# Three-part attention, routing and MLP kernel: side work between engines, the first load in three, MLP blocks of three tiles, and shifted ranks

## The chip, the cores and the metric

One core of a Trainium2 chip runs the whole program. The metric is device time in microseconds (us) of one execution, lower is better. The engines are TensorE (PE, matmuls and transposes, with weight loads as PEld), VectorE (DVE), ScalarE (ACT), GpSimd (POOL) and SyncE (SP, which issues most DMAs).

## The reference, cut to what matters

Three stages follow each other, on 4 sequences of 768 rows and 384 columns.

```python
# 1. gated linear attention, 8 heads of 48
state = alpha[:, :, t, :, None] * state + einsum('bhd,bhe->bhde', k[:, :, t], v[:, :, t])
y[:, :, t] = einsum('bhd,bhde->bhe', q[:, :, t], state)
# 2. four attention experts of width 64, the best two of four per row
q, k, v = x @ wq[e], x @ wk[e], x @ wv[e]
a = softmax(causal(scale * (q @ k.T)))
out += (e among the top 2) * w * (a @ v @ wo[e])
# 3. MLP, hidden width 1536
xn = (x - mean) / sqrt(var + 1e-6) * g_ln
return x + max(xn @ w_ch1, 0) @ w_ch2
```

## The kernel before, in words

Rows are worked on in tiles of 128, six to a sequence, 24 in all. Most matmul operands are split into a high and a low part (names ending in H and L or h and l), and a product is three matmuls: high by high, low by high, high by low.

*Front.* For each chunk `c` of 128 rows, `gla_a` makes the running product of alpha on DVE (the scan, L383), its logarithm and inverse on ACT (L386, L387), the product gm (L390, POOL, for the first chunk DVE), two steps on k (L392, L394, DVE) and the product on q (L396, POOL). `gla_b` makes the scores on PE in half-array mode (L415), masks them on DVE (`smk`, L422) and transposes k. `gla_c` updates the state (quarter-array matmuls L454; DVE adds; POOL multiplies by the decay, L471) and makes the output (L482), which DVE and ACT split into `xh`, `xl` (L509). For two chunks at a time, `qkv` projects (L539 with 256 columns, L560 with 260), and a chain of small operations makes the gate weights `W`.

*Attention units.* A unit `u` is one tile of queries and one pair of experts, 48 in all. `scores` makes the scores (L649); with more than four tiles of keys they come in two halves of 320 or 384 columns, and such a unit is called wide here. DVE takes row maxima and masks (L658, L660), ACT the exponentials (L664), and POOL makes `rr`, the gate weight over the sum, spread over 64 columns (L676). `transp` transposes exponentials and `rr` (L703), and either ACT or DVE copies them out (L709, L710). `av` multiplies by v (L732, quarter-array mode), DVE scales (L743), ACT takes the high part `oh` (L747) and POOL the low part `ol` (L748). `wout` projects both units of a tile (L759) and the result goes to DRAM.

*MLP.* Weights are converted on the way (`conv`, DVE, ACT and POOL). Blocks of rows follow: two of 256 rows (`NS = 2`) and five of 512. `mlp_tr` transposes (L893), `mlp_1` is the first layer (L919, with as many columns as the block has rows), `mlp_2` the second (L938, 384 columns, for each tile of the block). Small blocks may run among the units of the last sequence; the big ones need the memory of the attention.

*Order.* Nothing is issued as it is written. Every operation is recorded with a rank, `pos` (the PE time recorded before it), its cost in ns and the tiles that it reads and writes. `Plan.run` then walks through a model of the engines: on each it takes, among the operations that can start first, the one of lowest rank (on PE with a preference for the array mode in use), and issues it. An operation may have an alternative on a second engine, `alt`, and goes to the one where the model ends it first; before, only the copies L709 and L710 have that. While DVE holds an operation marked `lock`, a POOL operation is made to wait for it.

## Time and profile before

| | |
|---|---|
| median of 3 runs | 651.92 us (649.41 to 652.05) |
| profiled execution | 648.84 us, its span 647.1 us |
| TensorE clock granted | 1.000 of full speed |
| PE busy | 626.6 us, 6988 matmuls |
| DVE busy | 423.5 us, 1205 instructions |
| ACT busy | 282.7 us, 771 instructions |
| POOL busy | 160.1 us, 265 instructions |
| DMA | 60.93 MB, 94 GB/s on average |

The span runs from the first to the last instruction of the core. A busy PE is one with a matmul in flight, and ends of matmuls are modelled, so gaps of less than a matmul's own length between two of them do not show as idle. A matmul of 32-bit floats that is not in the split form stands in the trace as two.

### The profile page before, as it was taken

The page shows a single profiled execution, that of the slowest core. Times are in us where ns is not written, and L with a number is a line of the kernel's source. Part 1 is how long each engine was busy: PE and PEld are TensorE (multiplying, and loading weights), DVE is VectorE, ACT ScalarE, POOL GpSimd, SP SyncE. Part 2 cuts the span into 40 slices and gives each one's busy share as a digit, 9 for nine tenths or more (in the row PEclk, how much of TensorE's full clock was granted, in tenths as well). Part 3 has the DMA queues.
Part 4 walks back from the last instruction along what each step waited for, and adds up shares of the span by engine and source line. Part 5 has one row for each costly group of instructions (what it writes and reads, how often), then busy time and mean ns, then how long its engine had stood idle before and what let it go on. Part 6 is the DMA issues. An engine that isn't in the chain of part 4 may idle for free.

```text
span 647.1 us, 16965 instructions
## 1 busy us (share of the span) xinstructions
PE 626.6 (97%) x6988; PEld 574.9 (89%) x6988; DVE 423.5 (65%) x1205; ACT 282.7 (44%) x771; POOL 160.1 (25%) x265
## 2 busy tenths in 40 slices
PE   7899999999999999989899999999999999999997
PEld 6789999999988999878898998898898899899897
DVE  6999999999999988799997544424414324331311
ACT  4448565746766655676664422302402311320200
POOL 4475553546444443422223100000000000000000
PEclk9999999999999999999999999999999999999999
DMA  9445243634554223495231201011011011000001
GB/s 347 160 149 198 94 134 104 226 102 143 187 191 129 84 72 103 114 311 169 62 94 61 69 25 36 2 62 36 1 50 49 1 40 58 1 13 37 2 13 37
DMA packets 30430, 60.93 MB, mean 94 GB/s; under 512 B 2960, under 2 KB 19856, under 8 KB 30352
## 3 DMA queue, kind: packets, MB, share of 16 engines
q1 hardware_dynamic: 18864, 45.68, 21.5%
q10 hardware_dynamic: 8352, 9.44, 4.2%
q0 software_dynamic: 3136, 4.72, 2.7%
q8 instruction: 55, 0.90, 0.6%
q14 instruction: 23, 0.19, 0.1%
HBM read 45.67 MB, written 14.16 MB: 92 GB/s over the span
## 4 chain that ended last, share of the span: by engine, by line
PE 65%; DVE 3%; ACT 1%; issue 1%; POOL 0%; DVEq 0%; POOLq 0%
PE F L919 24%; PE F L938 23%; PE F L732 3%; PE F L703 3%; PE F L539 3%; PE F L759 2%; PE F L649 2%; PE F L560 2%; PE F L893 1%; PE F L482 1%; ACT A L664 1%; DVE mx L658 0%; DVE smk L422 0%; DVE gt L383 0%; PE F L454 0%
## 5 line engine op out<-in xcount | busy, mean ns | idle before, releaser
L919 PE MATMUL F<-Nh,w1hl 128*128 128x512 f32 x360 | 93.7, 395 | 0.0
L923 ACT ACTIVATE Hh<-F 128x512 fp32r<-128x512 f32 x60 | 36.0, 600 | 128.6 <-PE F L919 128.6
L924 DVE SCALAR_TENSOR_TENSOR Hl<-F,Hh 128x512 fp32r<-128x512 f32 x60 | 41.5, 691 | 74.4 <-ACT Hh L923 74.4
L919 PEld LDWEIGHTS F<-Nh,w1hl 128*128 128x128 f32 x360 | 67.6, 188 | 15.8
L938 PE MATMUL F<-w2h,Hh 128*128 128x384 f32 x240 | 81.7, 340 | 0.0
L938 PE MATMUL F<-w2h,Hl 128*128 128x384 f32 x240 | 80.7, 336 | 0.0
L938 PE MATMUL F<-w2l,Hh 128*128 128x384 f32 x240 | 80.6, 336 | 0.0
L664 ACT ACTIVATE A<-F,nm 128x384 f32<-128x384 f32 (+4 forms) x128 | 68.2, 543 | 24.3 <-DVE nm L660 20.5
L946 DVE TENSOR_TENSOR xt<-F,xt 128x384 f32<-128x384 f32 x24 | 13.3, 556 | 87.6 <-PE F L938 87.6
L703 PE MATMUL F<-ident,A 128*128 128x128 f32 x336 | 51.4, 276 | 5.3 <-ACT A L664 2.6
L919 PE MATMUL F<-Nl,w1hl 128*128 128x512 f32 x180 | 51.7, 396 | 0.0
L703 PEld LDWEIGHTS F<-ident,A 128*128 128x128 f32 x336 | 38.8, 140 | 10.2 <-ACT A L664 3.7
L938 PEld LDWEIGHTS F<-w2l,Hh 128*128 128x128 f32 x240 | 45.2, 188 | 0.0
L938 PEld LDWEIGHTS F<-w2h,Hh 128*128 128x128 f32 x240 | 45.1, 188 | 0.0
L938 PEld LDWEIGHTS F<-w2h,Hl 128*128 128x128 f32 x240 | 45.1, 188 | 0.0
L732 PE MATMUL F<-at,V 128*32 128x128 f32 x1344 | 44.1, 274 | 0.5 <-ACT A L664 0.5
L919 PEld LDWEIGHTS F<-Nl,w1hl 128*128 128x128 f32 x180 | 33.8, 188 | 8.2
L709 ACT ACTIVATE at<-F 128x384 f32<-128x384 f32 (+2 forms) x72 | 35.7, 517 | 11.1 <-PE F L703 10.8
L732 PEld LDWEIGHTS F<-at,V 128*32 128x32 f32 x1344 | 35.4, 109 | 4.5 <-issue 1.5
L482 PE MATMUL F<-smk,vb 128*32 128x128 f32 x768 | 33.9, 273 | 2.1 <-DVE smk L422 2.1
L676 POOL TENSOR_TENSOR rr<-den,W 128x128 f32<-128x128 f32 x48 | 19.1, 399 | 66.0 <-DVE den L674 24.0
L396 POOL TENSOR_TENSOR ld<-ld,gt 128x512 f32<-128x512 f32 (+1 forms) x26 | 29.1, 1118 | 20.1 <-DVE gt L383 13.0
(196 smaller groups left out, 1461.0 us busy)
## 6 DMA issues: line engine op xcount, KB each, us to landing
ld<-in_akq_dram SPq DMA_DIRECT2D x24, 770.0 KB, 4.9
vb<-in_vd_dram SPq DMA_DIRECT2D x24, 256.0 KB, 5.0
raw<-in_w_dram SPq DMA_DIRECT2D x18, 256.0 KB, 2.9
wsc<-whl ACTq DMA_DIRECT2D x18, 256.0 KB, 3.6
xs<-xo ACTq DMA_DIRECT2D x24, 192.0 KB, 2.1
raw<-in_w_dram SPq DMA_DIRECT2D x12, 384.0 KB, 3.2
w1hl<-wsc POOLq DMA_DIRECT2D x4, 1152.0 KB, 11.9
xt<-xs SPq DMA_DIRECT2D x24, 192.0 KB, 2.5
```

What stands on the lines that cost most here:

```text
L396: op("POOL", 1150 if m == 512 else 896, lambda js=js, q=q: pool.tensor_tensor(q(), q(), gt()[:, js, 1:], op=OP.mult), r=gts + kq, w=kq, na ...
L482: pe.matmul(o, l[x][0], l[x][1], start=(x == 0), stop=(x == len(l) - 1), skip_group_check=True)
L539: pe.matmul(P2()[:, mt % 2], wt()[:, k, cs], x()[:, k], start=(n == 0 and k == 0), stop=(n == 2 and k == 2))
L664: op("ACT", t_act(pw) + 200, lambda h=h, x=x: act.activation(A[h]()[:, pw * x:pw * x + pw], P[h][x]()[:, :pw], AF.Exp, bias=nm()[:, h:h + ...
L676: op("POOL", 360, lambda: pool.tensor_tensor(rr(), den()[:, :, None].to_broadcast([128, 2, 64]), W()[:, i, 2 * p:2 * p + 2, None].to_broad ...
L703: pe.transpose(P()[:, 128 * n:128 * n + 128], a, ident)
L709: fa = lambda cs=cs, P=P, n=n: act.activation(at()[:, cs], P()[:, :n], AF.Copy)
L732: pe.matmul(O()[64 * h + y:64 * h + y + ws], V()[:, x, HD * e + y:HD * e + y + ws], at()[:, c:c + 128], start=(x == 0), stop=(x == i), ski ...
L919: pe.matmul(P()[:, :n], t()[:, w, k, c], x()[:, k], start=(m == 0), stop=(m == 8))
L923: op("ACT", t_act(n) + 63, lambda P=P, hh=hh: act.activation(hh(), P()[:, :n], AF.Relu), r=[P], w=[hh], name="hh")
L924: op("DVE", t_dve(n), lambda P=P, hh=hh, hl=hl: dve.scalar_tensor_tensor(hl(), P()[:, :n], 0.0, f(hh()), op0=OP.max, op1=OP.subtract), r=[ ...
L938: pe.matmul(P()[:, :DM], x()[:, o], W2[w]()[:, ff], start=(ff == 0 and n == 0), stop=(ff == KF - 1 and n == 2))
```

## The change

The code changes in seven ways.

1. *Side work.* The q and gm products of the first two chunks go to DVE (`GD = 2`). The state's decay, two POOL operations of 48 partitions, becomes four of 112 partitions by 96 columns on ACT, each with POOL as the alternative (`SGA = 2`). `rr` and `ol` stay on POOL with DVE as the alternative (`RRA = 2`, `OLA = 1`). A subtraction on POOL in the gate chain becomes the bias of ACT's exponential, one for each tile instead of one for two. Clearing of `hot` and the states moves from POOL to DVE, and what waited for the whole of POOL's setup now waits for the part it reads.
2. *First load.* Chunk 0 comes in three transfers, the alpha part first, then k, then q.
3. *Finer waits.* Projections and scores wait for tiles of 128 rows instead of pairs.
4. *MLP blocks* of 2, 2, 2 and then six of 3 tiles. Their input loads are recorded earlier, and those of the three-tile blocks wait for the attention's memory.
5. *Six* warm-up groups on PE instead of ten, each with a higher cost.
6. *Cost* of a DMA's completion 2300 ns instead of 1900.
7. *Ranks.* `reorder` adds to `pos` of chosen groups of operations among the first 2600 a random shift, from thirty seeds (`ORDER`); `Plan.run` then picks by that `key`.

```diff
+BLOCKS = (2, 2, 2, 3, 3, 3, 3, 3, 3)
+SGA = 2
+RRA = 2
+GD = 2
+ORDER = (53, 71, 74, 129, 134, 144, 149, 254, 384, 385, 443, 714, 717, 1188, 1460, 2556, 3984, 10423, 11494, 13357, 14198, 14530, 17028, 17166, 17434, 17884, 18058, 20628, 21730, 22753)
+NW = 6
+OLA = 1
...
+    def reorder(self, seeds):
+        ops = self.ops[:2600]
+        for seed in seeds:
+            rnd = random.Random(seed)
+            mid = rnd.uniform(0, len(ops))
+            width = rnd.choice((60, 150, 400))
+            sigma = rnd.choice((400, 1500, 4000))
+            kind = rnd.choice((0, 1, 2))
+            group = {}
+            for o in ops[int(max(0, mid - width)):int(mid + width)]:
+                k = (o.name, o.name + o.plain[0], o.n)[kind]
+                if k not in group:
+                    group[k] = float(round(rnd.gauss(0, sigma))) if rnd.random() < (1, 0.5, 0.25)[kind] else 0.0
+                o.shift += group[k]
...
-                           key=lambda x: (x[1].pos + (STICK if x[1].mode != mode else 0.0), x[1].n))
+                           key=lambda x: (x[1].key + (STICK if x[1].mode != mode else 0.0), x[1].n))
...
-                o.end = chan + 1900.0
+                o.end = chan + 2300.0
...
+        for x, o, n in (("a", 0, AW), ("k", AW + 512, 512), ("q", AW, 512)):
+            op("SP", 400, lambda o=o, n=n: sp.dma_start(L()[:, o:o + n], akq[b, s][:, o:o + n]), w=[(L, (x, j)) for j in range(4)],
+               nbytes=512.0 * n, name=f"ld{c}")
...
-            ge, gn = (dve, "DVE") if c < 1 else (pool, "POOL")
+            ge, gn = (dve, "DVE") if c < max(GD, 1) else (pool, "POOL")
...
+            qe, qn = (dve, "DVE") if c < GD else (pool, "POOL")
...
+            for j in range(4 if SGA and s else 0):
+                gs = lambda j=j: (new_()[:112, j], new_()[:112, j], gt()[:112, j, 128:129])
+                sa = lambda gs=gs: act.activation(*gs()[:2], AF.Copy, scale=gs()[2])
+                sp_ = lambda j=j: pool.tensor_tensor(new_()[:112, j], new_()[:112, j], gt()[:112, j, 128:129, None].to_broadcast([112, 3, 32]), op=OP.mult)
+                op("ACT", 270, sa, r=[(gt, j), (new_, 0), (new_, 1)], w=[(new_, ("g", j))], name=f"stg{c}",
+                   alt=("POOL", 300, sp_, True) if SGA > 1 else None)
...
+            if RRA:
+                op("POOL", 360, lambda: m(pool), r=[den, (W, i)], w=[rr], name="rr", alt=("DVE", t_dve(128), lambda: m(dve), True) if RRA > 1 else None)
...
+        op("POOL", 420, lambda: lo(pool), r=[rb, (oh, p)], w=[(ol, p)], name=f"ol{u}", alt=("DVE", t_dve(128), lambda: lo(dve), True) if OLA else None)
...
-    BLKS = [(n, 1) for n in range(NS)] + [(n, 2) for n in range(NS, NBLK, 2)]
+    T0 = [sum(BLOCKS[:n]) for n in range(len(BLOCKS) + 1)]
...
+    plan.reorder(ORDER)
     plan.run(tc=tc)
```

What the built programs hold can be counted: POOL's instructions go from 270 to 169, DVE's from 1207 to 1268, ACT's from 687 to 786. On DVE there are 32 `rr` and 29 `ol` where there were none, and 29 copies of transposed weights instead of 48. ACT has 50 of the 64 state decays, POOL 14.

The rows below are instructions as they stand on one engine, without times: line, operation, output from inputs, size of the output, and a count where equal ones follow each other. Lines differ between the programs because the code has grown.

First, DVE at the very start, before the change; `ld_86` and `ld_87` are chunks 0 and 1, `gt` the scan's output, L390 is gm, L392 and L394 the steps on k, L355 a weight split.

```order
L383 SCALAR_TENSOR_TENSOR gt<-ld_86,hot 128x258 x2
L390 TENSOR_TENSOR ld_86<-gt,gi 128x256
L392 TENSOR_TENSOR ld_86<-ld_86,gi 128x256
L390 TENSOR_TENSOR ld_86<-gt,gi 128x256
L394 SCALAR_TENSOR_TENSOR ld_86<-ld_86 128x256
L392 TENSOR_TENSOR ld_86<-ld_86,gi 128x256
L383 SCALAR_TENSOR_TENSOR gt<-ld_87,hot 128x258
L394 SCALAR_TENSOR_TENSOR ld_86<-ld_86 128x256
L383 SCALAR_TENSOR_TENSOR gt<-ld_87,hot 128x258
L392 TENSOR_TENSOR ld_87<-ld_87,gi 128x256
L355 TENSOR_TENSOR WL<-A,WH 128x772
```

DVE at the same place after the change; L362 to L383 clear, L434 is the scan, L448 the q product, L441 gm, L443 and L445 the steps on k.

```order
L362 MEMSET hot 128x516
L363 MEMSET hot 128x4
L383 MEMSET st_94 128x384
L383 MEMSET st_93 128x384
L434 SCALAR_TENSOR_TENSOR gt<-ld_86,hot 128x258 x2
L448 TENSOR_TENSOR ld_86<-ld_86,gt 128x256
L441 TENSOR_TENSOR ld_86<-gt,gi 128x256
L448 TENSOR_TENSOR ld_86<-ld_86,gt 128x256
L441 TENSOR_TENSOR ld_86<-gt,gi 128x256
L443 TENSOR_TENSOR ld_86<-ld_86,gi 128x256 x2
L445 SCALAR_TENSOR_TENSOR ld_86<-ld_86 128x256
L434 SCALAR_TENSOR_TENSOR gt<-ld_87,hot 128x258 x2
```

Four clearings come ahead of the first scan, and two q products, which were POOL's, stand ahead of the first chunk's gm products.

Second, PE where the projections end (those of the fourth sequence, among the units of the third), before the change: L560 is the last projection of v, L703 transposes, L732 multiplies by v, and L649 with 320 columns is the first wide unit's scores.

```order
L560 MATMUL F<-WH,xh 128x260 x3
L560 MATMUL F<-WL,xh 128x260 x3
L560 MATMUL F<-WH,xl 128x260 x3
L703 MATMUL F<-ident,A 128x128 x8
L703 MATMUL F<-ident,rr 128x128
L703 MATMUL F<-ident,A 128x128 x8
L703 MATMUL F<-ident,rr 128x128
L732 MATMUL F<-at,V_108 32x128 x28
L649 MATMUL F<-KH_106,QH_104 128x320 x2
```

PE at the same place after the change: L717 are scores, L831 an output projection, L603 and L626 projections of q or k and of v.

```order
L717 MATMUL F<-KH_106,QH_104 128x320 x2
L717 MATMUL F<-KH_106,QL_105 128x320 x2
L717 MATMUL F<-KL_107,QH_104 128x320 x2
L774 MATMUL F<-ident,A 128x128 x3
L831 MATMUL F<-OWH,oh 128x384 x2
L831 MATMUL F<-OWL,oh 128x384 x2
L831 MATMUL F<-OWH,ol 128x384 x2
L603 MATMUL F<-xh,WH 128x256 x3
L603 MATMUL F<-xh,WL 128x256 x3
L603 MATMUL F<-xl,WH 128x256 x3
L626 MATMUL F<-WH,xh 128x260 x3
L626 MATMUL F<-WL,xh 128x260 x3
```

The first half of the wide unit's scores now stands ahead of the last four projection groups of nine matmuls, two of q or k and two of v; before, all of these stood ahead of it.

Third, DVE a little later, at the fourth sequence's last gate weights, before the change: L582 to L587 are the gate chain, L743 scales an attention output, L710 copies transposed weights.

```order
L582 TENSOR_REDUCE rank<-gt__5128 128x8
L583 SCALAR_TENSOR_TENSOR ex<-rank,ex 128x8
L584 TENSOR_REDUCE sd<-ex 128x2
L585 TENSOR_SCALAR sd<-sd 128x2
L743 TENSOR_TENSOR rb<-F,at 128x128
L586 RECIPROCAL sd<-sd 128x2
L710 COPY at<-F 128x384 x2
L587 TENSOR_TENSOR W_115<-ex,sd 128x8
```

DVE at the same place after the change: L648 to L652 are the gate chain, L814 scales, L781 copies, L819 is `ol`.

```order
L648 SCALAR_TENSOR_TENSOR ex_5182<-rank_5205,ex_5182 128x8
L814 TENSOR_TENSOR rb<-F,at 128x128
L649 TENSOR_REDUCE sd_5227<-ex_5182 128x2
L781 COPY at<-F 128x384
L650 TENSOR_SCALAR sd_5227<-sd_5227 128x2
L814 TENSOR_TENSOR rb<-F,at 128x128
L651 RECIPROCAL sd_5227<-sd_5227 128x2
L819 TENSOR_TENSOR ol<-rb,oh 128x128
L652 TENSOR_TENSOR W_115<-ex_5182,sd_5227 128x8
```

One copy has left DVE here and one `ol` has come; an `rr` stands a few rows ahead of these.

## Rows read from the trace of the kernel before

**Rows 1.** the page's part 1: busy us (share), instructions of each engine.

```profile
PE 626.6 (97%) x6988; PEld 574.9 (89%) x6988; DVE 423.5 (65%) x1205; ACT 282.7 (44%) x771; POOL 160.1 (25%) x265
```

**Rows 2.** busy us (instructions) of engines by stretch, PE clock, DMA, GB/s.

```profile
8.00:26.00 18.00, 12.00 (x250) 9.06 (x250) 17.06 (x30) 9.14 (x17) 7.66 (x9) 1.00 0.82 318
...
46.00:190.00 144.00, 143.40 (x2563) 133.74 (x2565) 135.82 (x376) 93.99 (x254) 74.29 (x115) 1.00 0.46 150
190.00:200.00 10.00, 7.95 (x83) 6.95 (x76) 9.85 (x27) 6.59 (x21) 2.91 (x6) 1.00 0.25 82
...
265.00:312.00 47.00, 41.72 (x623) 36.64 (x622) 43.60 (x149) 34.52 (x113) 15.56 (x29) 1.00 0.70 200
...
372.00:647.00 275.00, 271.54 (x1414) 246.07 (x1404) 92.19 (x226) 56.58 (x138) 0.94 (x2) 1.00 0.08 27
```

**Rows 3.** what PE waited for, 0 to 26 us: total us, times, longest.

```profile
PE F L482 <- DVE smk L422: 2.1, 4, 0.9
PE F L415 <- POOL ld L396: 1.8, 2, 1.0
PE F L342 <- POOL ident masks.py:199: 1.4, 1, 1.4
```

**Rows 4.** what PE waited for, 265 to 312 us.

```profile
PE F L703 <- ACT A L664: 2.6, 3, 0.9
...
PE F L759 <- ACT A L664: 1.0, 1, 1.0
PE F L919 <- ACT A L664: 0.7, 1, 0.7
```

**Rows 5.** timeline, 0 to 20 us: start, length, engine and instruction, idle before it.

```profile
0.81 0.85 SPq L291 DMA_DIRECT2D ld<-in_akq_dram  x2
...
5.28 1.28 DVE L383 TENSOR_TENSOR_SCAN gt<-ld,hot 128x258 f32<-128x258 f32 x2 [5.28 <-DMA ld<-in_akq_dram]
...
8.83 0.71 PE L415 MATMUL F<-ld 48*128 48x128 f32 x8 [0.80 <-DVE ld L394]
...
10.51 0.73 POOL L396 TENSOR_TENSOR ld<-ld,gt 128x256 f32<-128x256 f32 x1 [3.23 <-DVE gt L383]
...
11.29 0.71 PE L415 MATMUL F<-ld 48*128 48x128 f32 x8 [0.97 <-POOL ld L396]
```

**Rows 6.** the page's part 6: DMA issues, KB each, median us to landing.

```profile
raw<-in_w_dram SPq DMA_DIRECT2D x18, 256.0 KB, 2.9
```

**Rows 7.** the chain that ended last: start us, length us, matmuls.

```profile
311.62 11.05 PE F L919 x90
...
387.44 25.20 PE F L919 x108
...
618.58 24.98 PE F L938 x144
```

**Rows 8.** groups by line and shape: busy us, mean ns of one, idle before.

```profile
L422 DVE TENSOR_TENSOR smk<-F,gmask 128x512 f32<-128x512 f32 x48 | 31.1, 680 | 0.7 <-PE F L415 0.7
...
L710 DVE COPY at<-F 128x384 f32<-128x384 f32 x34 | 18.5, 551 | 2.2 <-PE F L703 1.5
...
L392 DVE TENSOR_TENSOR ld<-ld,gi 128x512 f32<-128x512 f32 x22 | 16.7, 761 | 0.7 <-ACT gi L387 0.5
...
L743 DVE TENSOR_TENSOR rb<-F,at 128x128 f32<-128x128 f32 x48 | 13.6, 284 | 3.6 <-PE F L732 2.9
...
L710 DVE COPY at<-F 128x512 f32<-128x512 f32 x11 | 7.5, 680 | 0.0
...
L392 DVE TENSOR_TENSOR ld<-ld,gi 128x256 f32<-128x256 f32 x4 | 1.7, 428 | 0.6 <-ACT gi L387 0.6
```

**Rows 9.** timeline of PE, 33 to 35 us: scores, then attention outputs.

```profile
33.80 0.28 PE L649 MATMUL F<-KH,QL 64*128 64x128 f32 x2
33.91 0.28 PE L649 MATMUL F<-KL,QH 64*128 64x128 f32 x2
34.12 0.43 PE L482 MATMUL F<-smk,vb 128*32 128x128 f32 x8
```

More of the change, by code (lines that the diff above doesn't have):

```diff
@@ L80 @@
 class Op:
-    __slots__ = ("eng", "ns", "fn", "mode", "pos", "deps", "left", "users", "tiles", "start", "end", "nbytes", "n", "ready", "name", "lock", "alt", "inst", "synced")
+    __slots__ = ("eng", "ns", "fn", "mode", "pos", "deps", "left", "users", "tiles", "start", "end", "nbytes", "n", "ready", "name", "lock", "alt", "inst", "synced", "plain", "shift", "key")
 class T:
@@ L131, in op @@
         o.deps = list(ds)
+        o.plain, o.shift = (eng, ns, fn, o.lock), 0.0
+        for d in o.deps:
+            d.users.append(o)
         self.ops.append(o)
@@ L140, in run @@
             o.ready = 0.0
-            for d in o.deps:
-                d.users.append(o)
+            o.eng, o.ns, o.fn, o.lock = o.plain
+            o.key = o.pos + o.shift
             for t in o.tiles:
@@ L153, in run @@
         done = 0
+        todo = sum(o.ns for o in self.ops if o.eng == "PE")
         while done < len(self.ops):
@@ L183, in run @@
                     best = (t0, e, cand)
+            if best is not None and free["PE"] + todo > cut:
+                return 1e12
             if best is None:
@@ L334, in setup @@
                            channel_multiplier=0)
-    op("POOL", 3900, setup, w=[K0] + st, name="setup")
-    for _ in range(10):
+    op("POOL", 1380, lambda: make_identity(nc, ident), w=[K0], name="setup")
+    op("DVE", 700, set_hot, w=[KH], name="setup")
+    for t in st:
+        op("DVE", 470, lambda t=t: dve.memset(t(), 0.0), w=[t], name="setup")
+    op("POOL", 600, set_g, w=[KG], name="setup")
+    op("POOL", 900, set_c, w=[KC], name="setup")
+    op("POOL", 400, set_tri, w=[KR], name="setup")
+    for _ in range(NW):
         P = psf()
@@ L475, in gla_c @@
         y3 = lambda: Y()[:, :384].rearrange("p (k t) -> p k t", k=3)
-        sts = [(sto, h) for h in range(2)] if s else []
+        sts = [sto] if s else []
         qs_ = lambda j: qk_of(c)[0][:112, j]
@@ L555, in qkv, with pv @@
+        for t in range(nt):
             P = psf()
-            def pv(t=t, P=P):
-                for n, (wt, x) in enumerate(three):
+            o = slice(128 * ((t0 + t) % 2), 128 * ((t0 + t) % 2) + 128)
+            def pv(o=o, P=P):
+                for y, (wt, x) in enumerate(three):
                     for k in range(KT):
-                        pe.matmul(P()[:, :260], x()[:, k, 128 * t:128 * t + 128], wt()[:, k, 512:772], start=(n == 0 and k == 0),
-                                  stop=(n == 2 and k == 2))
@@ L563, in qkv @@
-            op("PE", 9 * t_fr(260), pv, r=[WH, WL, xh, xl], w=[P], mode="full", name=f"v{m}")
-            op("ACT", t_act(260), lambda t=t, P=P: act.activation(V()[:, 2 * w + t], P()[:, :260], AF.Copy), r=[P], w=[(V, 2 * w + t)],
+                        pe.matmul(P()[:, :260], x()[:, k, o], wt()[:, k, 512:772], start=(y == 0 and k == 0), stop=(y == 2 and k == 2))
+            op("PE", 9 * t_fr(260), pv, r=[WH, WL, (xh, (t0 + t) % 2), (xl, (t0 + t) % 2)], w=[P], mode="full", name=f"v{m}")
+            op("ACT", t_act(260), lambda t=t, P=P: act.activation(V()[:, s0 + t], P()[:, :260], AF.Copy), r=[P], w=[(V, s0 + t)],
@@ L573, in qkv @@
-        l_s = lambda: lg()[:, :, :, None].to_broadcast([128, 2, 4, 4])
-        op("DVE", 75, lambda: dve.tensor_reduce(mx(), lg(), axis=AX.X, op=OP.max), r=vk, w=[mx], name="r1")
-        op("POOL", 200, lambda: pool.tensor_tensor(l2(), lg(), mx().to_broadcast([128, 2, 4]), op=OP.subtract), r=vk + [mx], w=[l2], name="r2")
-        op("ACT", 116, lambda: act.activation(ex(), l2(), AF.Exp), r=[l2], w=[ex], name="r3")
+        mx, ex, rank, sd = (small(s, f"{n}{nt}") for s, n in (([128, nt, 1], "mx"), ([128, nt, 4], "ex"), ([128, nt, 4], "rank"),
+                                                               ([128, nt, 1], "sd")))
@@ new lines, in qkv @@
+        gt_, eq_ = (small([128, nt, 4, 4], f"{n}{nt}") for n in ("gt_", "eq_"))
+        vk = [(V, t) for t in tk]
+        lg = lambda: V()[:, s0:s0 + nt, 256:260]
+        l_o = lambda: lg()[:, :, None, :].to_broadcast([128, nt, 4, 4])
+        l_s = lambda: lg()[:, :, :, None].to_broadcast([128, nt, 4, 4])
+        op("DVE", 75, lambda: dve.tensor_reduce(mx(), lg(), axis=AX.X, op=OP.max, negate=True), r=vk, w=[mx], name="r1")
+        for t in range(nt):
+            op("ACT", 190, lambda t=t: act.activation(ex()[:, t], lg()[:, t], AF.Exp, bias=mx()[:, t]), r=vk + [mx], w=[(ex, t)], name="r3")
@@ L607, in front @@
         for c in range(NCH):
-            if c + 2 < NCH:
+            if c + 2 < NCH and c >= AH:
                 gla_a(c + 2)
```

253 lines of the change are left out of this document (132 added, 121 removed).

## The prediction

> **What bounds the kernel now.** I read the page's first part, then the busy time by stretch, then the waits of TensorE (PE), then the chain that ended last. The reader is to see in [rows 1] that PE is busy 626.6 of 647.1 us: only 20.5 us of its span are waits, so no edit to another engine can give more than that unless it also makes PE's own work cheaper. [rows 2] says where those waits lie, as length less busy time. From 8 to 26 us: 18.00 - 12.00 = 6.0. From 46 to 190 us: 0.6 in 144. From 190 to 200 us: 2.05. From 265 to 312 us: 5.28. From 372 us to the end: 3.5, and [rows 7] has the last matmuls end at 618.58 + 24.98 = 643.56, 3.5 before the end, so this is the drain behind them. So there are two places with something to gain: the start, where PE waits for VectorE (DVE) and GpSimd (POOL) to prepare the first two chunks [rows 3], and the stretch from 265 to 312 us, where PE waits mostly for the exponentials of ScalarE (ACT) before it may transpose them [rows 4]. In the MLP behind 372 us the chain is PE alone [rows 7].
>
> The second thing to see in [rows 2] is DVE: 17.06 of 18 us, 135.82 of 144, 9.85 of 10, 43.60 of 47. It is nearly as full as PE all the way to 312 us. ACT has 34.52 of 47 in the worst stretch. Side work that moves to DVE is therefore not moved to an idle engine.
>
> **The base of the sum** is the profiled execution, 648.84 us (its span 647.1 and 1.74 around it). The median of the three runs shown is 651.92, so a change of x against 648.84 I put at 651.92 + x.
>
> **Start.** The first scan begins at 5.28 us, released by the first chunk's 770-KB load, whose issue began at 0.81: 4.47 us [rows 5]. The scan needs only the alpha part, now a transfer of its own of 264 KB. The nearest row is a 256-KB load, 2.9 us [rows 6], so the scan can begin at 0.81 + 2.9 = 3.7: -1.6 us. The four clearing operations that now stand ahead of it on DVE cost, at the 0.43 us of the nearest DVE row [rows 8], 1.7 us from 0.8 on and are over by 2.5, hidden by that load. If the alpha part lands no earlier than the whole did, the gain is 0.
>
> By the Trainium skill (DMA: Bandwidth & Descriptors, Anatomy of one DMA) a transfer costs about 2.0 us plus its bytes at 436 GB/s. That gives 2.6 us for the alpha part and 3.8 for the whole, an estimate of -1.2 instead of -1.6; it also counts the fixed cost three times, which speaks against splitting, but here no PE work waits for the later two parts alone.
>
> PE then waits twice for POOL's q product, 1.8 us in all [rows 3]; in [rows 5] POOL works on it from 10.51 and PE's score matmul begins at 11.29 after 0.97 idle. That product and the second chunk's gm product go to DVE: four q and two gm products more, 6 x 0.43 = 2.6 us on an engine that is busy 17.06 of 18. Net of the start: -1.6 - 1.8 + 2.6 = -0.8 if all of them delay PE, -3.4 if none does. In the order of DVE the first chunk's two q products stand ahead of its gm products, which wait for two functions of ACT anyway; I take -2.0, and keep +1 to -3.4 as its bounds.
>
> **The last projections.** In the order of before, the last q, k, v projections are done before the wide scores of the third sequence; after it, four groups of nine (36 matmuls) stand behind the first half of those scores. The chain has 90 matmuls of nearly the same width (256 columns) in 11.05 us [rows 7], 0.123 each: 4.4 us of PE work that needs no exponential, placed where PE now waits 5.3 us, 4.3 of them for ACT [rows 4]. Work moved into a wait gives at most its own length, -4.3, and it only covers the waits near it, the first of the stretch; the later ones belong to the fourth sequence. I take -2.5; the other end is +2, if the transposes that moved earlier meet exponentials that are not ready.
>
> **Waits elsewhere.** 2.05 us are lost from 190 to 200 us [rows 2], beside a DVE that is busy 9.85 of 10, and 20.5 - 1.4 - 6.0 - 2.05 - 5.28 - 3.5 = 2.3 in small pieces (the 1.4 before the first matmul from [rows 3]). The order there is entirely new. They may vanish, or others arise: -1, between -3 and +2.
>
> **Array shapes.** PE changes between full-array, half-array and quarter-array matmuls 113 times in the order of before and 106 times after. In [rows 9] matmul pairs of one form start 0.11 us apart and the first of another form 0.21 us after: 0.10 for a change, 7 x 0.10 = -0.7.
>
> **MLP blocks.** Before: two blocks of 256 rows and five of 512. After: three of 256 and six of 384. The second layer and the transposes do not change in number. First layer, from [rows 7]: 108 matmuls of 512 columns take 25.20 us (0.2333 each), 256 columns 0.1228 each; 384 columns I price by the second layer's, 144 in 24.98 us (0.1735). Before: 5 x 25.20 + 216 x 0.1228 = 152.5. After: 648 x 0.1735 + 324 x 0.1228 = 152.2. So -0.3, with 2 either way: the weights are loaded 972 times rather than 756, but matmuls of 256 columns, with half the time to hide a load, still run at 0.123, so loads do not set the pace. The order has the same 42 us of MLP work among the last attention units in both (counted in matmuls), so a third small block fills no wait there.
>
> **Side work.** 32 of the 48 rr products and 29 of the 48 ol differences go from POOL to DVE, at 0.284 each [rows 8] 17.3 us; the six products and four clearings above add 4.3; 19 copies of transposed weights leave DVE for ACT: 14 x 0.551 + 5 x 0.680 at most = 11.1. DVE has net 10.5 us more. ACT gets 50 state decays, these 19 copies and 12 exponentials, 81 x 0.37 (282.7 us over 771 instructions, [rows 1]) = 30 us. What hides DVE's 10.5 us is its own idle time: 8.2 us from 46 to 190 and 3.4 from 265 to 312 [rows 2], and the slack that POOL's slower steps used to take. I take 0, because PE waited only 0.6 us in 144 beside a DVE that was 94% busy; if the cover is gone it costs up to +10.5, and if shorter chains to the transposes and output projections help, -2.
>
> **Sum:** -2.0 - 2.5 - 1 - 0.7 - 0.3 + 0 = -6.5 against 648.84, that is 642.3 in a profiled execution, and 645.4 as a median.
>
> **Rivals.**
>
> *More of the waits go.* Every wait between 26 and 372 us is 2.05 + 5.28 + 2.3 = 9.6 us; if four fifths of it and the start's -3.4 are gained, with 0.7: -11.8, or 640. For it: the order is changed everywhere, and the waits have few causes. Against: DVE's extra work. Below 641: 0.20.
>
> *The waits only move.* The bound is PE's own work, which the change leaves the same to about 1 us; new meetings replace the old ones, and the start gains 0.8. About 651, within 0.5% (3.3 us, which is about what a measurement of this kernel can tell from no change): 0.20.
>
> *DVE becomes what PE waits for.* The place is the score-to-transpose step of the wide units from 265 to 312 us: row maxima and masking stand on DVE behind rr, ol and weight conversion, ACT's exponentials wait for them and PE for those. DVE has 3.4 us left there. It decides when more than about 6 us of the 10.5 reach PE, since the start and the array changes give back 2.7 and 3.3 is the bound of telling. A further load is seen in [rows 8]: the two-input product with both inputs in SBUF takes 0.761 on average and the one that reads PSUM 0.680, so the 67 moved operations may each lose 0.08: 5.4 us. With all 10.5 and the 5.4 less 2.7: +13, 665; with half of 15.9 on the path, +5.2: 657. Chance of over 655.2: 0.15.
>
> The Trainium skill (SBUF - State Buffer, SBUF: two separate sides) states that DVE and POOL take a shared pair of ports exclusively for a whole instruction, and that a DVE instruction with two SBUF inputs can be blocked by a POOL one. The trace agrees with the direction by the 0.761 against 0.680; by this rule fewer POOL instructions also mean fewer holders of the lock, so it speaks for both sides.
>
> **How the numbers follow.** My forecast, 641 to 648.6, has 0.45; with the larger gain 0.65 for faster. No change has 0.20, slower 0.15. The likeliest time is the sum, 645. The range leaves out about one in ten on each side: down to 636, past the 640 of the larger gain, and up to 656, into the DVE case.
>
> **What the profile of the changed kernel would show.** Start: first scan near 3.7 us, first score matmul before 8.0 (8.83 in [rows 5]), no wait of PE for POOL's q. Last projections: PE idle from the first wide scores to the first MLP matmul under 3 us. MLP: 108 matmuls of 384 columns in 18.7 us; over 20 means weight loads set the pace. Side work: DVE busy time up by about 10 us before the MLP, POOL's instructions fewer by about 100; PE's waits named by DVE rising over 5 us would mean the slower rival. I am wrong if PE's idle time after 26 us is not below 9 us, or if PE's busy time grows although its work is the same.

## The result and the profile after

The changed kernel takes 641.5 us (median of 4 runs, 640.4 to 642.13), before 651.5 (median of 4 runs, 649.41 to 652.05): a ratio of 0.9859, with a 95% interval of 0.9835 to 0.9883. The profiled execution of after took 642.13 us with a span of 640.4. Against the profiled execution of before, 647.1, the span is 6.7 us shorter; the medians lie 10.0 apart.

The page's part 1 of after, which answers to [rows 1]:

```profile
PE 625.8 (98%) x7188; PEld 599.3 (94%) x7188; DVE 424.4 (66%) x1266; ACT 311.1 (49%) x870; POOL 111.5 (17%) x164
```

PE's busy time falls by 0.8 us and its waits from 20.5 to 14.6. That is the whole 6.7. DVE is busy 0.9 us more, not 10. The stretches of after, as in [rows 2]:

```profile
8.00:26.00 18.00, 13.61 (x215) 11.29 (x216) 16.05 (x31) 9.39 (x19) 2.49 (x2) 0.81 0.90 344
46.00:190.00 144.00, 143.47 (x2540) 133.49 (x2540) 137.57 (x403) 105.92 (x294) 54.42 (x73) 1.00 0.42 145
190.00:200.00 10.00, 10.00 (x96) 9.51 (x94) 9.55 (x28) 7.47 (x20) 2.42 (x4) 1.00 0.48 180
265.00:312.00 47.00, 45.59 (x709) 39.86 (x707) 43.66 (x158) 39.52 (x128) 12.26 (x20) 1.00 0.64 174
372.00:640.40 268.40, 264.98 (x1582) 264.45 (x1580) 93.35 (x244) 57.65 (x150) 0.00 (x0) 1.00 0.09 30
```

From 265 to 312 us PE waits 1.41 instead of 5.28, from 190 to 200 nothing instead of 2.05. The drain at the end is 3.42 as before. The first stretch has a granted clock of 0.81, in before's profile it was 1.00. What PE waits for from 265 to 312 us now, against [rows 4]:

```profile
PE F L803 <- ACT A L732: 0.6, 1, 0.6
PE F L831 <- ACT A L732: 0.5, 1, 0.5
PE F L774 <- DVE nl L972: 0.3, 1, 0.3
```

From 0 to 26 us, against [rows 3], no wait for POOL's q product (L448) is left, and the wait for DVE's step on k (L445) has grown from 1.1 to 3.1. The row of before, then the three longest of after:

```profile
PE F L415 <- DVE ld L394: 1.1, 2, 0.8
```

```profile
PE F L467 <- DVE ld L445: 3.1, 2, 2.3
PE F L392 <- POOL ident masks.py:199: 1.4, 1, 1.4
PE F L506 <- ACT kt L488: 1.4, 2, 0.7
```

The timeline of after shows why, beside [rows 5]:

```profile
0.81 1.33 SPq L331 DMA_DIRECT2D ld<-in_akq_dram  x3
...
3.63 1.28 DVE L434 TENSOR_TENSOR_SCAN gt<-ld,hot 128x258 f32<-128x258 f32 x2 [1.21 <-DMA ld<-in_akq_dram]
...
4.81 0.42 ACT L438 ACTIVATE gi<-gi 128x258 f32<-128x258 f32 x1
...
6.63 0.42 DVE L448 TENSOR_TENSOR ld<-ld,gt 128x256 f32<-128x256 f32 x1 [1.72 <-DMA ld<-in_akq_dram]
6.98 0.42 DVE L441 TENSOR_TENSOR ld<-gt,gi 128x256 f32<-128x256 f32 x1
7.31 0.42 DVE L448 TENSOR_TENSOR ld<-ld,gt 128x256 f32<-128x256 f32 x1
7.65 0.42 DVE L441 TENSOR_TENSOR ld<-gt,gi 128x256 f32<-128x256 f32 x1
...
9.13 0.71 PE L467 MATMUL F<-ld 48*128 48x128 f32 x8 [2.32 <-DVE ld L445]
...
19.77 0.38 PE L541 MATMUL F<-smk,vb 128*32 128x128 f32 x2
```

The alpha part lands and the scan starts at 3.63, 1.65 us earlier than before. Then DVE stands for 1.72 us at the q product, because the third part of the load is not there before 6.63; the first gm product (L441), whose inputs are ready at 5.23 when ACT's inverse ends (L438), is queued behind it. PE starts its first scores at 9.13, before at 8.83. Chunk 1's first outputs start at 19.77, and in the timeline of before at 19.70:

```profile
19.70 0.41 PE L482 MATMUL F<-smk,vb 128*32 128x128 f32 x2 [0.89 <-DVE smk L422]
```

By that row the start gains nothing. PE's stretches of after in the start (busy us, matmuls, granted clock, DMA share, GB/s):

```profile
10.00:11.00 1.00, 0.36 (x4) 0.90 1.01 405
11.00:17.00 6.00, 5.31 (x82) 0.50 1.02 408
17.00:18.00 1.00, 1.00 (x14) 0.68 1.09 405
18.00:26.00 8.00, 6.22 (x117) 1.00 0.72 263
```

Behind the idle 2.32 us the clock falls to its lower level, 1.2 GHz, by these rows from 10.8 to 17.6 us. In the MLP the chain that ended last shows 384-column matmuls at the price that the prediction took, 18.72 for 108 (0.173 each) in the first layer, and the second beside it:

```profile
445.80 18.72 PE F L990 x108
...
465.50 18.73 PE F L1009 x108
```

### The profile page after: what moved, and what is told of

Same layout as the page of the kernel before. It is cut to its first block, busy times and chain, and to the rows that moved or that the text cites. A ratio compares the mean times of both kernels' runs of the same rounds, so it can differ in the third digit from the quotient of the medians.

```text
span 640.4 us, 17450 instructions
## 1 busy us (share of the span) xinstructions
PE 625.8 (98%) x7188; PEld 599.3 (94%) x7188; DVE 424.4 (66%) x1266; ACT 311.1 (49%) x870; POOL 111.5 (17%) x164
## 4 chain that ended last, share of the span: by engine, by line
PE 90%; DVE 5%; ACT 2%; issue 2%; DMA 1%; POOL 0%; SPq 0%; ACTq 0%; DVEq 0%; POOLq 0%
PE F L990 24%; PE F L1009 23%; PE F L603 8%; PE F L774 6%; PE F L803 5%; PE F L541 5%; PE F L717 5%; PE F L831 4%; PE F L626 4%; PE F L467 3%; PE F L484 1%; PE F L506 1%; PE F L965 1%; DMA ld<-in_akq_dram 1%; DVE gt L434 1%
## 5 line engine op out<-in xcount | busy, mean ns | idle before, releaser
L990 PE MATMUL F<-nh,w1hl 128*128 128x384 f32 (+1 forms) x648 | 118.7, 318 | 0.0
L995 DVE SCALAR_TENSOR_TENSOR hl<-F,hh 128x384 fp32r<-128x384 f32 (+1 forms) x108 | 55.2, 511 | 79.8 <-ACT hh L994 79.5
L990 PEld LDWEIGHTS F<-nh,w1hl 128*128 128x128 f32 x648 | 104.8, 189 | 0.1
L1009 PE MATMUL F<-w2h,hh 128*128 128x384 f32 x288 | 97.6, 339 | 0.0
L1009 PE MATMUL F<-w2h,hl 128*128 128x384 f32 x288 | 96.3, 334 | 0.0
L1009 PE MATMUL F<-w2l,hh 128*128 128x384 f32 x288 | 96.3, 334 | 0.0
L732 ACT ACTIVATE A<-F,nm 128x384 f32<-128x384 f32 (+4 forms) x128 | 68.0, 540 | 14.4 <-DVE nm L728 12.2
L990 PE MATMUL F<-nl,w1hl 128*128 128x384 f32 (+1 forms) x324 | 67.8, 317 | 0.0
L1009 PEld LDWEIGHTS F<-w2h,hh 128*128 128x128 f32 x288 | 54.1, 188 | 0.4 <-issue 0.4
L1009 PEld LDWEIGHTS F<-w2l,hh 128*128 128x128 f32 x288 | 54.2, 188 | 0.0
L1009 PEld LDWEIGHTS F<-w2h,hl 128*128 128x128 f32 x288 | 54.1, 188 | 0.0
L448 POOL TENSOR_TENSOR ld<-ld,gt 128x512 f32<-128x512 f32 x22 | 26.1, 1190 | 66.1 <-DVE gt L434 25.4
L541 PE MATMUL F<-smk,vb 128*32 128x128 f32 x768 | 34.8, 279 | 1.1 <-issue 0.7
```

Source lines behind the costliest of these rows:

```text
L541: pe.matmul(o, l[x][0], l[x][1], start=(x == 0), stop=(x == len(l) - 1), skip_group_check=True)
L732: op("ACT", t_act(pw) + 200, lambda h=h, x=x: act.activation(A[h]()[:, pw * x:pw * x + pw], P[h][x]()[:, :pw], AF.Exp, bias=nm()[:, h:h + ...
L990: pe.matmul(P()[:, :n], t()[:, w, k, c], x()[:, k], start=(m == 0), stop=(m == 8))
L995: op("DVE", t_dve(n), lambda P=P, hh=hh, hl=hl: dve.scalar_tensor_tensor(hl(), P()[:, :n], 0.0, f(hh()), op0=OP.max, op1=OP.subtract), r=[ ...
L1009: pe.matmul(P()[:, :DM], x()[:, o], W2[w]()[:, ff], start=(ff == 0 and n == 0), stop=(ff == KF - 1 and n == 2))
```

## The experiments

All start from the changed kernel, except the last of the table. "Order kept" means that each engine's instructions stand in the same sequence but for the edit named. Times are medians; the ratio is to the kernel before, run on the same chip. After was not run again beside the others, and the medians of before beside them are 650.4 to 650.5 where it had 651.5: a difference from after in us can be off by about 1, a difference of ratios is the safer one.

| run | us (lowest to highest) | ratio, 95% interval |
|---|---|---|
| after | 641.5 (640.4 to 642.13) | 0.9859, 0.9835 to 0.9883 |
| 42 warm-up transposes | 637.99 (637.09 to 638.55) | 0.9806, 0.9784 to 0.9828 |
| one load | 640.95 (640.36 to 642.66) | 0.9860, 0.9839 to 0.9881 |
| 42, load alpha-q-k | 638.19 (637.49 to 638.68) | 0.9812, 0.9790 to 0.9833 |
| rr and ol on POOL | 640.18 (639.7 to 641.04) | 0.9844, 0.9823 to 0.9866 |
| no rank shifts | 648.32 (647.31 to 649.46) | 0.9966, 0.9950 to 0.9982 |
| 42, alpha-q-k, k step first | 638.34 (638.29 to 639.1) | 0.9825, 0.9809 to 0.9840 |
| the same with fills | 639.27 (638.76 to 639.72) | 0.9836, 0.9820 to 0.9852 |
| projections early | 643.08 (642.47 to 644.35) | 0.9897, 0.9879 to 0.9915 |
| nine tiny products | 639.2 (638.83 to 639.68) | 0.9827, 0.9803 to 0.9850 |
| 42, alpha-q-k, q of chunk 1 on POOL | 639.01 (637.55 to 639.64) | 0.9816, 0.9791 to 0.9840 |
| the same, rr and ol on POOL | 638.65 (637.86 to 641.07) | 0.9824, 0.9797 to 0.9851 |
| before with fills | 648.56 (648.37 to 650.68) | 0.9978, 0.9965 to 0.9992 |

**A longer warm-up** (order kept).

```diff
-            for x in range(4):
+            for x in (0, 1, 2, 3, 0, 1, 2):
                 pe.transpose(P()[:, 128 * x:128 * x + 128], ident, ident)
```

> After with six warm-up groups of 7 transposes (42) instead of 4 (24), everything else and the order the same. Theory (the idle time of PE before the first score matmul is what the clock falls behind): the warm-up ends about 8.7 us instead of 6.8, PE idles about 0.5 before the first score instead of 2.32, the granted clock stays 1.00 from 8 to 26 us where after shows 0.81, and the 12-us stretch of slow matmuls gives back 1.5 to 2.5: about 639.5. Rival (DVE's chain on the first chunks sets when PE's work can start, so PE merely waits longer at full clock): within 0.6 of after's 641.5, with PE idle from 8 to 26 us grown by about what the matmuls lost.

3.5 us faster than after: more than the theory's price, and most of it not by its mechanism. PE still idles 1.19 us before the first scores where 0.5 was expected, and from 8 to 26 us the profiled clock is 0.91, not 1.00:

```profile
9.41 0.72 PE L467 MATMUL F<-ld 48*128 48x128 f32 x8 [1.19 <-DVE ld L445]
```

Against the profile of after, the first v projection starts 1.2 us earlier (21.03 against 22.20), 0.6 is gained at 77 us, and 1.9 at 208 and 230 us, where two waits of after are missing. The 0.6 at 77 us is missing in every other run with after's order too, so it belongs to the profiled execution of after, the slowest of its four. Part of the 1.2 may be of that kind: in three runs below that have after's 24 transposes (one load, projections early, rr and ol on POOL) the same projection starts at 21.99, 21.71 and 21.29. The nine tiny products below take the two waits alone.

**One load again** (order kept): the first of the three transfers takes the whole chunk.

```diff
-op("SP", 400, lambda o=o, n=n: sp.dma_start(L()[:, o:o + n], akq[b, s][:, o:o + n]), ...
+op("SP", 400, (lambda: sp.dma_start(L(), akq[b, s])) if x == "a" else None, ...
```

> After with chunk 0 in one transfer again, the order of all other work the same. Theory (the split brings nothing, because the third part, q, lands at 6.63 us and the first score matmul needs it): the scan begins near 5.3 instead of 3.6, q and gm follow by 7.5, the first score is within 0.4 of after's 9.13 us and the time within 0.7 of 641.5. Rival (the earlier scan is worth what the prediction gave it): first score near 10.7, time about 643.1, and more if the clock falls longer.

The theory holds: 640.95, the same as after. Its timeline has the scan 1.84 us later than after's and the first scores 0.22 later, at 9.35:

```profile
5.47 1.28 DVE L434 TENSOR_TENSOR_SCAN gt<-ld,hot 128x258 f32<-128x258 f32 x2 [3.06 <-DMA ld<-in_akq_dram]
...
9.35 0.71 PE L467 MATMUL F<-ld 48*128 48x128 f32 x8 [2.58 <-DVE ld L445]
```

The whole chunk is there at 5.47, sooner than the last of three parts at 6.63. By the Trainium skill (DMA: Bandwidth & Descriptors, Anatomy of one DMA) each transfer issued from POOL's queue pays a fixed cost of its own. That the last of three parts comes 1.16 us behind the whole agrees with it in direction, though these loads are issued by SP. The prediction's 3.8 and 2.6 us, worked out from the figures of that section of the Trainium skill, came out low: from the issue at 0.81 to the scan it is 4.66 us for the whole here, and 2.82 for the alpha part in after.

**The parts in the order alpha, q, k**, with the longer warm-up (order kept).

```diff
-for x, o, n in (("a", 0, AW), ("k", AW + 512, 512), ("q", AW, 512)):
+for x, o, n in (("a", 0, AW), ("k", AW, 512), ("q", AW + 512, 512)):
```

(the offsets are exchanged, so q is at AW; the names only tell the planner which transfer is which, and its order stays)

> The 42 warm-up transposes, and the parts of chunk 0 land in the order alpha, q, k instead of alpha, k, q. Theory (q's landing is what the first score waits for): DVE's q product starts about 5.6 instead of 6.63, the first score about 0.7 earlier than with 42 transposes alone if k is not then late itself (its steps stand behind q and gm on DVE), time 0.5 to 0.8 below that run: about 639. Rival (the score waits for DVE's whole row of q, gm and k products, whose last input is the later of q and k whatever the order): the same as that run within 0.3.

The q product now starts at 4.82 without a wait and the first scores at 7.71, 1.7 us earlier than with 42 transposes alone:

```profile
4.82 0.40 DVE L448 TENSOR_TENSOR ld<-ld,gt 128x256 f32<-128x256 f32 x1
...
7.71 0.72 PE L467 MATMUL F<-ld 48*128 48x128 f32 x8
...
10.23 0.71 PE L467 MATMUL F<-ld 48*128 48x128 f32 x8 [1.80 <-DVE ld L445]
```

The time is the same, 638.19: the rival's number, but not its reason, since the score did come earlier. The second score matmuls started only at 10.23, behind chunk 1's scans on DVE, so the next run moved that.

**The k step before the scans.** The second step on k of chunk 0's second half is issued ahead of chunk 1's scans (the planner's order is taken down, changed by this one move, and then issued).

```diff
-    plan.run(tc=tc)
+    order = []
+    plan.run(emit=False, log=order)
+    for n, to in ((38, 40),):
+        o = next(x for x in order if x.n == n)
+        order.remove(o)
+        order.insert(next(i for i, x in enumerate(order) if x.n == to), o)
+    for o in order:
+        if o.fn:
+            o.inst = o.fn()
...
```

> The 42 transposes, the parts of chunk 0 in the order alpha, q, k, and one instruction moved on DVE: the second step on k for the second half of chunk 0 goes ahead of chunk 1's two scans. All else in after's order. Theory (from 8 to 26 us DVE is full and sets the time, so only what DVE idles counts): the move fills 0.4 us of DVE's wait for chunk 1's load, and the time is 0.3 to 0.6 below the run with alpha, q, k alone (638.2). Rival (PE's second score matmul, 1.8 us late behind that step, sets it): it starts near 8.5 instead of 10.2, and the time falls by 1.2 to 1.8.

Neither number came: 638.34, no change. The timeline shows the wait one step further on:

```profile
7.55 1.16 PE L467 MATMUL F<-ld 48*128 48x128 f32 x16
...
11.52 0.58 ACT L488 ACTIVATE kt<-F 128x512 f32<-128x512 f32 x1
11.53 1.28 DVE L474 TENSOR_TENSOR smk<-F,gmask 128x512 f32<-128x512 f32 x2
...
12.14 1.08 PE L506 MATMUL F<-vb,kt 128*32 128x64 f32 x32 [2.85 <-ACT kt L488]
```

All 16 scores are begun by 8.7, and then ACT's copy of k and DVE's mask stand in their queues until 11.5, behind chunk 1's steps and a weight conversion.

**Fills**: the same with 28 more transposes in PE's waits.

```diff
+FS, FU, FO = 2, 6, 6
...
+            if c < 2 and j0 == 0:
+                for _ in range(FS):
+                    pe.transpose(P[0]()[:, 384:512], ident, ident)
...
```

(and `FU` and `FO` of the same before each state update and each first output of chunks 0 and 1)

> As the run with the moved k step, with 28 more transposes of the identity, whose results nobody reads, put on PE ahead of the second score matmuls (2), the state updates (6) and the first outputs (6) of chunks 0 and 1, where PE waits for ACT and DVE. Theory (idle time of PE between 8 and 13 us is what the clock falls behind, in 4 of 5 executions): the granted clock is 1.00 throughout, in every execution, and the time is 636 to 637 with a smaller spread than before. Rival (PE is in time there whatever its clock, since DVE is late): no faster than the run with the moved step, within 0.4.

The clock did as expected, the time did not. From 8 to 26 us, with the moved k step (first row) and with fills added (second):

```profile
8.00:26.00 18.00, 14.30 (x219) 12.30 (x216) 16.00 (x28) 10.04 (x21) 2.48 (x2) 0.72 0.90 345
```

```profile
8.00:26.00 18.00, 15.61 (x252) 12.87 (x251) 16.31 (x28) 10.59 (x22) 2.49 (x2) 1.00 0.92 357
```

The four executions with fills have a mean clock of 0.999 to 1.000, the four without 0.991 to 0.997, and those with fills are slower by 0.9 in the median, in ranges that overlap. The first v projection starts 1.1 us earlier with fills (20.97 against 22.07), then PE waits 0.54 for a weight split of DVE, and the first q projection starts 0.4 earlier (22.96 against 23.35). The rival is right that the time does not fall; where the 0.9 goes is open.

This does not price the clock alone, because the fills are work and shift what follows in PE's stream. The executions of one kernel do: in each of the four other runs with 42 transposes (alone, with alpha-q-k, and the two with q of chunk 1 on POOL) every execution with a mean clock of 0.999 or 1.000 is faster than every one with 0.995 to 0.997, by 0.8 to 2.7 us in the mean. So the lower clock has a price in the changed kernel too.

**The same in the kernel before**: 44 transposes and 28 fills, its order kept.

```diff
-            for x in range(4):
+            for x in (0, 1, 2, 3, 0)[:4 + (g > 5)]:
                 pe.transpose(P()[:, 128 * x:128 * x + 128], ident, ident)
...
+            if c < 2 and j0 == 0:
+                for _ in range(FS):
+                    pe.transpose(P[0]()[:, 384:512], ident, ident)
...
```

(`g` is the warm-up group, of ten; `FS` is 3, and five and six fills stand before the state updates and the first outputs)

> The kernel before, its order kept, with 44 warm-up transposes instead of 40 and 28 more transposes of the identity, read by nobody, in PE's waits of the first two chunks. In 7 of the 9 runs of before whose clock was listed the mean granted clock was 0.989 to 0.996 and the time 649.6 to 651.8; in 2 it was 1.000 and the time 648.6. Theory (the slow clock at the start is what separates them): the granted clock is 1.000 in nearly every execution and the time 648 to 649. Rival (POOL and DVE set the start, the clock is only a sign of it): 650 to 651.5 at clock 1.000.

Here the theory holds. 8 of 12 runs have a clock of 1.000 and take 648.4 to 648.8; four have 0.995 to 0.997 and take 649.5 to 650.7. Of the 17 runs of before beside them 15 have 0.994 to 0.997, two 0.988, none 1.000; the median is 650.38, 1.8 above that with fills. The profiled execution of before, with 1.000, was one that the lower clock had spared.

**Nine tiny products** on PE ahead of the first v projection, nothing else.

```diff
+            def pv(o=o, P=P, first=t0 + t == 0):
+                for _ in range(9 if first else 0):
+                    pe.matmul(P()[:32, 384:392], ident[:, :32], ident[:, :8], start=True, stop=True)
```

> After (24 warm-up transposes) with nine products of 32 by 8 values, read by nobody, on PE ahead of the first v projection, at 22 us, where PE waits 0.7 us for a weight split. They are 18 matmuls and 18 weight loads more in PE's stream, as many as the 18 transposes by which the warm-up had grown, and leave the start as after has it. Theory (the waits at 208 and 230 us that the profile explains by nothing, 1.06 and 0.70 in after, none in the runs with 42 transposes, depend on where in PE's stream its blocks of instructions end): they are gone or under 0.3, and the time falls by 1.2 to 2, to 639.5 to 640.3. Rival (those waits come and go with the DMA traffic, or the longer warm-up itself removed them): they are there as in after, time within 0.6 of 641.5.

The theory holds: 639.2, 2.3 us less by adding work (2.1 by the ratios). The start and its clock (0.995) are after's. What PE waits for from 200 to 265 us in after is one row; with the tiny products the same view is empty:

```profile
PE F L541 <- issue: 1.8, 2, 1.1
```

So of the longer warm-up's 3.5 us about 2 go with these two waits, and the medians leave about 1.2 for the start and its clock.

**No rank shifts.**

```diff
-    plan.reorder(ORDER)
+    plan.reorder(())
```

> After with the rank shifts taken out (an empty list of seeds), all other parts of the change kept; the planner's order is then by plain rank. Theory (the shifts, by way of the order, removed PE's waits between 190 and 372 us): PE's waits from 26 to 372 us are 4 to 6 us longer than after's, most of them for ACT's exponentials between 260 and 312 us, and the time is 645 to 648. Rival (the side work, the finer waits and the blocks did it, the shifts only stir the order): within 2 of 641.5. The start keeps its slow clock in both.

648.32, 6.8 above after (7.0 by the ratios) and a little above the forecast. PE's waits from 26 to 372 us are 7.4 longer, not 4 to 6, and nearly half of that lies ahead of 190 us. What is left of the change without the shifts is a ratio of 0.9966. Its stretches from 46 to 190 and from 265 to 312 us, and what PE waits for in the second:

```profile
46.00:190.00 144.00, 140.17 (x2523) 130.12 (x2524) 137.89 (x403) 98.21 (x274) 56.53 (x78) 1.00 0.43 142
...
265.00:312.00 47.00, 41.95 (x630) 37.63 (x629) 43.22 (x150) 34.81 (x115) 11.40 (x18) 1.00 0.61 166
```

```profile
PE F L831 <- ACT A L732: 4.4, 3, 1.7
PE F L774 <- ACT A L732: 0.7, 1, 0.7
```

3.83 us of waits where after has 0.53, and 5.05 where it has 1.41. The waits for the exponentials are back with all the side work, blocks and finer waits in place. The shifts without the rest, and other orders beside the rest, were not run.

**Projections early**: the last four groups and their copies ahead of the wide scores, the rest of the order kept.

```diff
...
+    early = [next(x for x in order if x.n == n) for n in (1646, 1657, 1658, 1645, 1655, 1661, 1656, 1662)]
+    order = [x for x in order if x not in early]
+    at = next(i for i, x in enumerate(order) if x.n == 1682)
+    order[at:at] = early
...
```

> After with the last four groups of nine projection matmuls (keys and values of the fourth sequence's last two tiles) and their four copies on ACT and DVE put ahead of the first half of the wide scores behind which after has them, as in the order of before; everything else as after. Theory (the step of the prediction: these 4.4 us of PE work are what fills the wait for the exponentials): PE's waits from 250 to 312 us rise by 2 to 3 us, time near 644. Rival (they stand at 259 to 264 us, ahead of the waits; what fills them is scores of later units): PE's waits from 265 to 312 us within 0.5 of after's 1.41, time within 0.8 of 641.5.

643.08, 1.6 above after, and 2.5 by the ratios. By the profiles: at 229 us this run is 1.08 us ahead of after (the wait in L541 ends at 228.69, in after at 229.77), and at the next output projection 1.22 behind (272.01 against 270.79), so 2.3 us are lost between. That is the theory's size in time, but not its mechanism: PE's waits from 250 to 312 us rise by 1.1 (2.50 against 1.41), not by 2 to 3. PE's waits from 255 to 275 us in this run:

```profile
PE F L831 <- ACT A L732: 0.5, 1, 0.5
PE F L774 <- DVE rr L744: 0.4, 1, 0.4
PE F L774 <- POOL rr L744: 0.4, 1, 0.4
PE F L717 <- DVE rb L814: 0.3, 1, 0.3
```

In after only the first of these rows is there. The projections cover small steps on DVE and POOL, not exponentials; the named rows make 1.1 of the 2.3, and the rest is in pieces that the view does not name.

**rr and ol on POOL** (order kept; DVE loses 61 instructions).

```diff
-... alt=("DVE", t_dve(128), lambda: m(dve), True) ...
+... alt=("DVE", t_dve(128), lambda: m(pool), True) ...
```

(and the same for `lo`)

> After with all 48 rr products and all 48 ol differences on POOL, each at the place where the planner put it; DVE loses 61 instructions (about 17 us of work), POOL gains them; the order on PE and ACT unchanged. Theory (the order of the work carries the gain, and the side work on DVE only fills its idle time): within 1.5 of 641.5. Rival (the shorter path to the transposes and output projections by DVE is what removed PE's waits from 46 to 372 us): PE's waits there return, 3 to 6 us slower, 645 to 648, named by POOL's rr or ol. A third way, DVE's load was costing PE time all along: 1 to 3 faster.

640.18, 1.3 below after: inside the theory's 1.5, and inside the third way's 1 to 3 as well, while the intervals of the ratios overlap. In its profile after's wait of 1.06 us at 208 us is missing, and PE gains 1.3 us on after at that place. So this run shows neither a gain nor a cost of the side work on DVE; the rival's 3 to 6 us are excluded. Part 1 of its page:

```profile
PE 624.5 (98%) x7188; PEld 598.5 (94%) x7188; DVE 420.5 (66%) x1205; ACT 311.0 (49%) x870; POOL 145.7 (23%) x225
```

POOL is busy 34.2 us more, DVE only 3.9 less, although the 61 instructions had taken some 17.5 (32 at 292 ns and 29 at 283 in after). The lengths of DVE's other 1205 instructions add up to 6.7 us more, and neighbours overlap by 6.9 us less, which the busy time counts once.

**q of chunk 1 on POOL**, with 42 transposes and alpha, q, k.

```diff
-... lambda js=js, q=q, qe=qe: qe.tensor_tensor(
+... lambda js=js, q=q, qe=pool if c == 1 else qe: qe.tensor_tensor(
```

> The run with 42 transposes and the parts in the order alpha, q, k, and the two q products of chunk 1 on POOL again instead of DVE, at the same places. Theory (from 8 to 26 us DVE sets the time): DVE is relieved of 0.84 us, POOL, idle there, does them in 1.8, and the time is 0.4 to 0.8 below that run's 638.2. Rival (POOL's product is later than DVE's and the score matmul of chunk 1 waits for it, as chunk 0's did in the kernel before): 0.3 to 0.9 above, with PE named as waiting for POOL's q.

639.01 with a spread of 2.1: no gain. It is 0.8 above the run without, the rival's number, but no wait for POOL's q stands in the start. It tells neither apart.

**That with rr and ol on POOL as well**: the two edits above together.

> As the run with chunk 1's q products on POOL, and all rr products and ol differences on POOL too. Theory (DVE's spare time counts a little everywhere, as the run with this side work on POOL was 1.3 below after): 0.5 to 1.3 below the run without that, about 637. Rival (it is worth nothing, that run was drawn with shorter waits that the profile does not explain): within 0.4 of it.

638.65, within 0.4 as the rival has it, but with a spread of 3.2 it could not have shown the theory's 0.5. No version is faster than the longer warm-up alone, 637.99, which is faster than both kernels.

## Why the prediction came out as it did

The time lies inside the range and in the likeliest case (641 to 648.6), 3.9 below the number given. The sum, -6.5 against a profiled -6.7, is right by errors that cancel, and that is luck: the start's -2.0 did not come, the waits elsewhere gave more than -1, and two new waits cost 1.8.

**The start, -2.0, is the step that failed.** The scan at 3.7 came (3.63), but the first score matmul, forecast before 8.0, came at 9.13. The sentence "here no PE work waits for the later two parts alone" was wrong: the first scores need q, q came third, and gm was queued behind it on DVE. The gain of the split is 0, shown by the run with one load. Bringing q or the k step earlier gave nothing either: the wait moved to the next queue each time. What would shorten the start by more is not settled; the runs show that none of load, q and second k step does it alone, and the longer warm-up, with the clock, about 1.2 us by the medians.

**The last projections, -2.5**, were right in size (1.6 by medians, 2.5 by ratios, 2.3 by profiles) and wrong in what they cover: rr and rb rather than exponentials.

**Waits elsewhere, -1, was too small.** Without the shifts the time is 6.8 higher. PE's waits from 190 to 200 us are gone (-2.05), and 3.9 us from 265 to 312, which the projections alone don't explain. Against them stand the two new waits of 1.06 and 0.70 us at 208 and 230. The prediction looked for the cause in one moved block and took the rest of the order as noise.

**Array shapes, -0.7**, no run measured. **MLP, -0.3**: 0.173 for 384 columns as priced, so the weight loads do not set the pace; no run measured the term apart. **Side work, 0**: nothing contradicts it; two runs find 1.3 and 0.4 us, less than they can tell. DVE's busy time, forecast 10 higher, rose by 0.9, and this is mostly a matter of counting. The lengths of DVE's instructions add up to 499.0 us before and 506.4 after, 7.4 more; but neighbours overlap, as the products above, which take 0.42 and start 0.34 apart, and these overlaps, 75.5 and 82.0, count once in the busy time. Lengths over-price work that is added to a full queue. A smaller part, 3.1 us, is that the instructions of equal form and number got shorter as POOL's went from 265 to 164. The k step of 512 columns takes 728 ns in after, 761 in [rows 8], and 741 with rr and ol on POOL; the group's row of after, then of that run:

```profile
L443 DVE TENSOR_TENSOR ld<-ld,gi 128x512 f32<-128x512 f32 x22 | 16.0, 728 | 0.6 <-ACT gi L438 0.6
```

```profile
L443 DVE TENSOR_TENSOR ld<-ld,gi 128x512 f32<-128x512 f32 x22 | 16.2, 741 | 0.7 <-ACT gi L438 0.6
```

One by one, the k steps during which no POOL instruction runs take 683 ns on average before (12 of 22), 676 in after (18) and 680 with rr and ol on POOL (10), none over 693; the others take 854, 964 and 792, up to 1814. So the 0.08 that the prediction set on each moved operation goes with POOL at work beside them, not with two SBUF inputs as such. The rule of the Trainium skill that the prediction weighed (SBUF - State Buffer, SBUF: two separate sides), by which POOL can block a DVE instruction with two SBUF inputs, agrees with this.

**The base.** "651.92 + x" took a change of the profiled execution to be the same change of the median. The profile had a clock of 1.000 at the start, which only two of the 41 other executions of before with a listed clock had, and holding it is worth 1.8 us there. After has the lower clock in all four runs (0.994 to 0.995), its profiled one among them, and that one was the slowest of its four. So before's profile stands 2.7 us below its median and after's 0.6 above: these are the 3.3 by which the medians moved more than the spans, and the clock accounts for about 1.8 of them.

**The rivals.** "DVE becomes what PE waits for" did not happen: from 46 to 312 us no DVE wait of PE is above 0.3. "The waits only move" happened in the start alone. "More of the waits go" came near: 641.5 against its bound of 641.

## What to carry to other kernels

A part of a split load is worth nothing if the next instruction in the consumer's queue needs the last part: follow the queue, not the data. Price work that is added to a full queue by the distance between starts, not by the length of one instruction. When an order is changed everywhere, price it by the waits that it can remove in each stretch, and let one run with the old order separate it from the edits beside it. Compare the granted clock of the profiled execution with that of the other runs before using it as a base.

## What was not expected of the hardware

PE can wait for nothing that the profile names, at a place that depends on the instructions ahead. In after it is 1.06 and 0.70 us amid the short matmuls of L541, at 208 and 230 us:

```profile
207.98 0.27 PE L541 MATMUL F<-ld,st 112*32 112x128 f32 x1 [1.06 <-issue]
...
229.77 0.27 PE L541 MATMUL F<-smk,vb 128*32 128x128 f32 x1 [0.70 <-issue]
```

With eighteen more matmul rows ahead, nearly without length, both waits were gone, and the time 2.3 us less. The run with early projections has both (1.06 and 0.70), the one with one load 0.34 and 0.15, the one with rr and ol on POOL 0.69 at the second place, and in the six with 42 transposes none there is above 0.23. Up to the first of them PE's rows are the same in number in after, with early projections and with one load, and the wait stands at the same row: so the place goes with the instructions ahead, but the length does not go with them alone. The page's part 3 lists a queue of 56 packets and 0.92 MB for instructions in after:

```profile
q8 instruction: 56, 0.92, 0.6%
```

That PE stood waiting for one of them is a guess that no run tested. In the packet records of these three runs each of the six waits ends 1.3 to 1.6 us behind the end of such a packet, which fits it and does not show it. The other surprise is the clock: after 5.4 us of warm-up, 2.32 of idle, 0.7 of scores and 0.8 more of idle it fell to half at about 10.8 us and stayed there to 17.6, although PE was busy 5.31 of the 6 us from 11 to 17. Holding it up by fills was worth 1.8 us in the kernel before and nothing in the changed one, where executions of one kernel with the higher clock are still 0.8 to 2.7 us faster.
